# Second expert layer and output in two halves of 256 columns, with all combination weights kept in SBUF

## The chip, the cores and the metric

The kernel runs on one core of a Trainium2 chip. The metric is the device time of one execution in microseconds (us). The kernel before took 548.74 us (median of three runs, 547.72 to 548.89). The profile is of one execution, recorded by the hardware profiler.

Engines are named as the profile names them: PE is the matrix engine (PEld its weight loads), DVE the vector engine, ACT the scalar engine, POOL the GpSimd engine, SP the engine that issues the DMAs.

## The reference, cut to what matters

Thresholded attention over 8 batches, 8 heads, 576 positions, 64 dimensions a head. Its output, as `x` of 4608 tokens by 512 columns, goes through a soft mixture of 8 experts with 4 slots each:

```python
logits = x @ phi                        # 4608 x 32 slots
slot_input = softmax(logits, axis 0).T @ x          # 32 x 512
for e in range(8):
    h = np.maximum(slot_input[e] @ w1[e], 0.0)      # 4 x 1024
    slot_out[e] = h @ w2[e]                         # 4 x 512
c = softmax(logits, axis 1)             # the combination weights, 4608 x 32
return c @ slot_out                     # 4608 x 512
```

`w1` and `w2` are 8 x 1024 x 512 numbers of float32 each, 33.6 MB in all, and the output is 9.44 MB.

## The kernel before, in words

The attention and the slot inputs take the first 483 us, in an order that a planner inside the kernel computes. The change touches only what follows, the tail, whose order is written out by hand: every engine executes its part in program order.

**Weights.** The weights come in 64 units of 512 KB: units 0 to 31 are `w1` (four experts, 128 rows each), units 32 to 63 are `w2` (256 rows of one expert, two rows of 512 columns a partition, so that each partition reads 4 KB in one piece). 46 units fit into SBUF before the tail: 26 in the `w` buffers, loaded during the attention, and 20 in `host` buffers, which take the space of attention buffers as those die. The last `NX = 6` of them, units 12 to 17, lie where the tail's own tiles will lie. The last 18 units, 46 to 63, are loaded by `load_unit` (line 451) into buffers that `stage1` (line 993) and `stage2` (line 1024) have read.

**Layers.** `stage1(a, kb)` multiplies the slot inputs by four units of `w1`, four experts side by side in column groups of 32 on PE. `relu` and `hidden` turn the result into the stationary operand `hz`. `stage2(a, k)` does the second layer in eight steps, each of two rows by four experts; all steps add up in one PSUM tile `so` of 512 columns, and the last step, whose units arrive last, is done in two column halves (`end`). float32 matmuls are two instructions each.

**Combination.** `ct` (line 962) makes one of nine blocks `cT` of combination weights: POOL multiplies (`c_block`), PE transposes, ACT copies, DVE subtracts to split the numbers into two float32r parts. Two blocks are made before the second layer, seven among the output jobs; three buffers hold them. `combine` (line 1054) sums the experts' result over the groups (`sr`), splits it into `sh`, and runs 18 output jobs: two matmuls of 512 columns each (`o`), one result copied out by ACT and one by DVE, and a store of 512 KB in pieces of 4 KB. The last block's two jobs are each stored by two DMAs from 64 partitions.

**Queues.** All DMAs are issued by SP, in program order. `otile` hands out six PSUM tiles in turn for the outputs, three of which the transposes use too.

Of the kernel before, what the change touches and what calls it, by code (L numbers as in the profile page):

```python
# [10 lines left out]
F32 = mybir.dt.float32  # L11
F32R = mybir.dt.float32r
AF = mybir.ActivationFunctionType
ALU = mybir.AluOpType
# [8 lines left out]
    k=2, q=2, vv=2, r=3, ri=3, nmx=4, thr=4, p2=4, pL=1, pTa=1, pTb=1, pTl=1, l4=1,  # L23
# [8 lines left out]
NPRE = 26  # L32
# [3 lines left out]
NHOST = 20  # L36
TABLE = {}
for _n, _v in (
# [78 lines left out]
    TABLE.update({(_n, _i): _x for _i, _x in enumerate(_v) if _x is not None})  # L117
OFF = dict(qk=-1.0, mx=0.0, ex=0.3, th=0.4, st=1.0, ri=1.3, sc=1.5, tt=3.0, te=3.3, tl=3.5, tle=3.8, a0=2.0, a1=5.0,
           ae=0.5, x=6.0, xe=6.3, D=1.0)


class Buf:
# [215 lines left out]
def softmax_attention_soft_moe(  # L338
# [17 lines left out]
    nc = tc.nc  # L356
    B, HP, D, _, S = qT.shape
    NP = B * HP
    N9 = 9
    DM = out.shape[1]  # L360
    E, _, F = w1.shape
    NS = phi.shape[1]
    SPE = NS // E
    SM = 512
# [74 lines left out]
    NG = E // 4  # L439
# [1 line left out]
    units += [(1, 0, 4 * a + g, k) for a in range(NG) for k in range(4) for g in range(4)]  # L441
    wslots = [wp.tile([128, 1024], F32, name=f"w{i}") for i in range(NPRE)]

    NX = 6
    X = range(12, 12 + NX)
    n = NPRE + NHOST
    units = [(i, *units[i]) for i in (*range(X[0]), *range(X[-1] + 1, n), *X, *range(n, len(units)))]
    n_units = len(units)
    where = {}

    def load_unit(t):

        if len(where) == len(units):
            return
        i, kind, _, e, k = units[len(where)]
        where[i] = t
        if kind == 0:
            nc.sync.dma_start(t, w1[e, k * 128:(k + 1) * 128, :])
        else:
            nc.sync.dma_start(t, w2[e, k * 256:(k + 1) * 256, :].rearrange("(p j) f -> p (j f)", j=2))  # L460
# [478 lines left out]
    def ttile(name):  # L939
        return ps_t.tile([128, 512], F32, tag="t", name=name)  # L940

    def two(name, tag):

        return ttile(name + "a"), ps_h.tile([128, 512], F32, tag=tag, name=name + "b")
# [14 lines left out]
    blocks = [(slice(row(b), row(b) + 4), 4) for b in range(B)] + [(slice(N9 - 1, NR, N9), B // 2)]  # L959
    c4s, cTs = [], []  # L960

    def ct():


        if len(cTs) == len(blocks):
            return
        while len(c4s) < min(len(cTs) + 2, len(blocks)):
            c4s.append(c_block(*blocks[len(c4s)]))
        k = blocks[len(cTs)][1]
        c4 = c4s[len(cTs)]  # L970
        n = 128 * k
        t = tx.tile([128, SM], F32R, tag="cT", name=f"cT{len(cTs)}", bufs=3)
        if len(cTs) < 2:
            w = two(f"ct{len(cTs)}", "h00" if cTs else "h01")
            for i in range(k):
                split(w, i, c4[:, i].rearrange("p g s -> p (g s)"))
            tv = t.rearrange("p (i g q) -> p i g q", i=4, g=2)
            for g in range(2):
                wv = w[g][:, 0:256].rearrange("p (i q) -> p i q", i=4)
                nc.scalar.copy(tv[:, :, g], wv)  # L980
                nc.vector.tensor_tensor(
                    out=tv[64:128, :, g], in0=wv[64:128], in1=tv[64:128, :, g].bitcast(F32), op=ALU.subtract)
            cTs.append(t)
            return
        w = ttile(f"ct{len(cTs)}")
        for i in range(k):
            tr(w[:, i * 128:(i + 1) * 128], c4[:, i].rearrange("p g s -> p (g s)"))
        nc.scalar.copy(t[:, 0:n], w[:, 0:n])
        nc.vector.tensor_tensor(  # L989
            out=t[64:128, 0:n], in0=w[64:128, 0:n], in1=t[64:128, 0:n].bitcast(F32), op=ALU.subtract)  # L990
        cTs.append(t)

    def stage1(a, kb, hp):
        t = [where[a * 16 + kb * 4 + g] for g in range(4)]
# [17 lines left out]
    def hidden(a, hid):  # L1012
        for n in range(2):
            w = two(f"ht{a}_{n}", "h10" if a and n else "h00" if n else "h01")
            for k in range(4):
                split(w, k, hid[:, (n * 2 + k // 2) * 256 + k % 2:(n * 2 + k // 2 + 1) * 256:2])
            for g, m in enumerate(rows):
                nc.vector.tensor_tensor(
                    out=hz[:, a, n * 4:(n + 1) * 4, m], in0=w[g][:, 0:256].rearrange("p (k m) -> p k m", k=4),
                    in1=mask[:, a].rearrange("p g s -> p (g s)")[:, None, m].to_broadcast([128, 4, 64]),  # L1020
                    op=ALU.mult,
                )

    def stage2(a, k):
        t = [where[n_units // 2 + a * 16 + k * 4 + g].rearrange("p (j f) -> p j f", j=2) for g in range(4)]

        last = a == NG - 1 and k == 3
        for q, dst in enumerate(end if last else [so]):
            c = slice(q * DM // 2, (q + 1) * DM // 2) if last else slice(0, DM)
            for j in range(2):  # L1030
                for g in range(4):
                    nc.tensor.matmul(
                        dst[g * 32:(g + 1) * 32, 0:c.stop - c.start], hz[:, a, k * 2 + j, g * 32:(g + 1) * 32],
                        t[g][:, j, c], start=(j == 0 and (last or a == 0 and k == 0)),
                        stop=(j == 1 and (last or a == NG - 1 and k == 2)),
                        tile_position=(0, 32 * g), skip_group_check=True)
        for g in range(4):
            load_unit(where[n_units // 2 + a * 16 + k * 4 + g])

    cnt = [-1]  # L1040

    def otile(name):
        cnt[0] += 1
        k = cnt[0] % 6
        return ps_h.tile([128, 512], F32, tag=("h01", "h10", "h11")[k // 2], name=name) if k % 2 else ttile(name)

    def through():

        last = {}
        for i in set(range(n_units)) - set(X):  # L1050
            last[id(where[i])] = (i, where[i])
        return [t for i, t in sorted(last.values(), key=lambda x: x[0])]

    def combine():

        cols = [slice(n * DM // 2, (n + 1) * DM // 2) for n in range(2)]
        for q, w in zip(cols, end):
            nc.vector.tensor_tensor(out=so_sb[:, q], in0=w[:, 0:DM // 2], in1=so_sb[:, q], op=ALU.add)
        for q, x in enumerate(cols):
            w = ttile(f"sr{q}")  # L1060
            nc.tensor.matmul(w[:, 0:DM // 2], st4.rearrange("p g s -> p (g s)"), so_sb[:, x], start=True, stop=True)
            nc.scalar.copy(sh[:, x], w[:, 0:DM // 2])
            nc.vector.scalar_tensor_tensor(
                out=sh[:, x], in0=sh[:, x].bitcast(F32), scalar=neg, in1=w[:, 0:DM // 2], op0=ALU.mult, op1=ALU.add)
        free = through()

        jobs = [(b, k) for b in range(B) for k in (0, 2)] + [(B, k) for k in range(0, B // 2, 2)]
        ov = out.rearrange("(i h s) d -> h s i d", h=2, s=S)
        for n, (b, k) in enumerate(jobs):
            ot = free[n].rearrange("p (c d) -> p c d", c=2)  # L1070
            token = lambda c: slice(k + c, SM, 4) if b < B else slice((k + c) * 128, (k + c + 1) * 128)
            ws = [otile(f"o{n}_{c}") for c in range(2 if n else 0)]
            for q, x in enumerate(cols if n == 0 else []):
                for c in range(2):
                    w = otile(f"o{n}_{c}_{q}")[:, 0:DM // 2]
                    nc.tensor.matmul(w, cTs[b][:, token(c)], sh[:, x], start=True, stop=True)
                    if q:
                        nc.vector.tensor_copy(ot[:, c, x], w)
                    else:
                        nc.scalar.copy(ot[:, c, x], w)  # L1080
            for c in range(len(ws)):
                nc.tensor.matmul(ws[c], cTs[b][:, token(c)], sh, start=True, stop=True)
                if c == 0:
                    nc.scalar.copy(ot[:, c], ws[c])
                else:
                    nc.vector.tensor_copy(ot[:, c], ws[c])  # L1086
            if k:
                ct()
            if b < B:
                nc.sync.dma_start(  # L1090
                    out[b * S:b * S + SM].rearrange("(p c) d -> p c d", c=4)[:, k:k + 2], ot)
            else:
                for h in range(2):
                    nc.sync.dma_start(ov[h, SM:S, k:k + 2], ot[h * 64:(h + 1) * 64])

    hp = [[ps_h.tile([128, 512], F32, tag=f"h{a}{n}", name=f"h{a}_{n}") for n in range(2)] for a in range(NG)]
    hid = []
    so = ps_h.tile([128, 512], F32, tag="so", name="so")
    end = [None, None]
    for a in range(NG):  # L1100
        for kb in range(4):
            stage1(a, kb, hp[a])
# [11 lines left out]
        hid.append(relu(a, hp[a]))  # L1114
    ct()
    ct()
    end[:] = [ps_h.tile([128, 512], F32, tag=t, name=t + "e") for t in ("h00", "h11")]
    for a in range(NG):
        for k in range(4):
            if a == NG - 1 and k == 3:  # L1120
                so_sb = tx.tile([128, DM], F32, name="so_sb")
                nc.scalar.copy(so_sb, so)
            stage2(a, k)
            if a < NG - 1 and k == 1:
                hidden(a + 1, hid[a + 1])
    combine()
    order_all.close()


# [45 lines left out]
```

## Time and profile before

| | before |
|---|---|
| time, median of 3 runs | 548.74 us |
| span of the profiled execution, as its page gives it | 546.2 us |
| PE busy | 527.5 us (97%) |
| DVE, ACT, POOL busy | 471.0, 457.4, 242.1 us |
| HBM read, written | 72.42 MB, 9.44 MB |

The page gives no other time of the profiled execution than its span. Shares of busy time are averages over the whole run. The tail, 483 to 546 us, has limits of its own, and the rows further down are taken from there.

### The profile page before, as it was taken

The numbers are of one execution on the slowest core, as the hardware profiler recorded it, in microseconds if no ns is written. First come the engines' busy times: TensorE is split into PE (matmuls) and PEld (weight loads), VectorE is DVE, ScalarE is ACT, GpSimd is POOL, SyncE is SP. The second block draws the span as 40 slices with busy tenths as digits, with TensorE's granted clock in tenths as the row PEclk, the third lists the DMA queues.
The fourth block names the chain that finished last, engine by engine and source line by source line (L and its number), as shares of the span: only waits on it lengthen the run. The fifth ranks groups of instructions, "written<-read, shape, count | busy, mean of one in ns | idle before, by whom it ended". The sixth has DMA issues, their size and how long they took to land.

```text
span 546.2 us, 18324 instructions
## 1 busy us (share of the span) xinstructions
PE 527.5 (97%) x7029; PEld 337.0 (62%) x7029; DVE 471.0 (86%) x1332; ACT 457.4 (84%) x790; POOL 242.1 (44%) x475
## 2 busy tenths in 40 slices
PE   8999999999999999999999999999999999999990
PEld 6666666666666666666666666666666656644470
DVE  5999998999999999999899989999999999523192
ACT  3899998999899989999999989999999888621181
POOL 2554555554545464545355545545454524121030
PEclk9999999999999999999999999999999999999997
DMA  6355555565535543333333333333333322999498
GB/s 176 74 158 178 168 167 169 138 190 161 166 90 167 172 153 122 92 94 86 78 91 92 91 91 92 91 91 91 91 90 91 91 76 69 336 410 408 197 375 316
DMA packets 31990, 83.03 MB, mean 152 GB/s; under 512 B 4640, under 2 KB 12832, under 8 KB 31904
## 3 DMA queue, kind: packets, MB, share of 16 engines
q1 hardware_dynamic: 31904, 81.87, 48.8%
q8 instruction: 55, 0.90, 0.7%
q14 instruction: 31, 0.25, 0.2%
HBM read 72.42 MB, written 9.44 MB: 150 GB/s over the span
## 4 chain that ended last, share of the span: by engine, by line
PE 82%; DVE 5%; DMA 5%; ACT 4%; issue 2%; DVEq 0%; POOL 0%; SPq 0%; POOLq 0%; ACTq 0%
PE ps L670 29%; PE ps L552 24%; PE ps L478 17%; DMA w<-in_w 5%; PE ps L557 3%; PE ps L694 2%; PE ps L752 2%; PE ps L800 1%; DVE p L580 1%; PE up L418 1%; DVE cT L989 1%; DVE host L1086 1%; ACT pTa L483 1%; DVE ss L564 1%; PE ps L470 1%
## 5 line engine op out<-in xcount | busy, mean ns | idle before, releaser
L564 DVE TENSOR_SCALAR_CACHE_REDUCE ss<-ps 128x576 f32<-128x576 f32 x288 | 209.1, 752 | 15.5 <-ACT pTl L483 4.8
L577 POOL TENSOR_SCALAR thr<-nmx,pabs 128x1 f32<-128x1 f32 x288 | 132.2, 461 | 187.0 <-DVE ss L564 167.7
L580 DVE SCALAR_TENSOR_TENSOR p<-ss,thr,p 128x576 f32<-128x576 f32 x256 | 201.8, 823 | 3.4 <-ACT p L574 3.1
L574 ACT ACTIVATE p<-ss,nmx 128x576 f32<-128x576 f32 x256 | 188.2, 781 | 18.3 <-DVE ss L564 18.2
L552 PE MATMUL ps<-k,q 64*128 64x288 f32 x1024 | 167.2, 427 | 1.0 <-ACT pTb L483 0.4
L478 PE MATMUL ps<-ident,p 64*128 64x64 f32 x2304 | 98.2, 223 | 0.9 <-ACT pTa L483 0.3
L478 PEld LDWEIGHTS ps<-ident,p 64*128 64x128 f32 x2304 | 87.8, 138 | 17.8 <-issue 3.3
L552 PEld LDWEIGHTS ps<-k,q 64*128 64x128 f32 x1024 | 83.3, 188 | 21.9 <-ACT pTl L652 5.8
L483 ACT COPY pTb<-ps 128x1024 f32<-128x1024 f32 (+1 forms) x96 | 84.0, 876 | 5.7 <-PE ps L478 3.5
L670 PE MATMUL ps<-pTb,vv 128*64 128x320 f32 x512 | 76.0, 439 | 0.4 <-DVE pTl L652 0.4
L483 ACT COPY pTa<-ps 128x1024 f32<-128x1024 f32 x64 | 64.9, 1018 | 0.4 <-PE ps L478 0.4
L670 PE MATMUL ps<-pTa,vv 128*64 128x256 f32 x512 | 62.3, 385 | 0.0
L670 PEld LDWEIGHTS ps<-pTb,vv 128*64 128x64 f32 x512 | 34.1, 136 | 36.4 <-issue 9.0
L670 PEld LDWEIGHTS ps<-pTa,vv 128*64 128x64 f32 x512 | 33.9, 136 | 26.2 <-DVE ss L564 8.5
L670 PE MATMUL ps<-pTl,vv 128*64 128x256 f32 (+1 forms) x256 | 41.9, 406 | 0.0
L689 POOL TENSOR_TENSOR x<-x,ri 128x512 f32<-128x512 f32 x31 | 32.3, 1043 | 4.8 <-ACT x L483 4.8
L483 ACT COPY xT<-ps 128x256 f32<-128x256 f32 (+1 forms) x62 | 24.6, 398 | 6.2 <-PE ps L670 5.2
L670 PEld LDWEIGHTS ps<-pTl,vv 128*64 128x64 f32 x256 | 18.5, 137 | 12.6
L580 DVE SCALAR_TENSOR_TENSOR pL<-ss,thr,pL 128x576 f32<-128x576 f32 x32 | 26.0, 812 | 0.0
L574 ACT ACTIVATE pL<-ss,nmx 128x576 f32<-128x576 f32 x32 | 24.8, 776 | 0.4 <-DVE ss L564 0.4
L954 POOL TENSOR_TENSOR c<-lall,crow 128x512 f32<-128x512 f32 x9 | 9.3, 1046 | 35.7 <-PE ct L470 21.4
L483 ACT COPY pTl<-ps 128x256 f32<-128x256 f32 x64 | 24.2, 378 | 0.4 <-PE ps L478 0.4
(165 smaller groups left out, 550.3 us busy)
## 6 DMA issues: line engine op xcount, KB each, us to landing
w<-in_w SPq DMA_DIRECT2D x44, 512.0 KB, 7.3
q<-in_qT SPq DMA_DIRECT2D x62, 288.0 KB, 4.5
vv<-in_vt SPq DMA_DIRECT2D x32, 320.0 KB, 4.6
host<-in_w SPq DMA_DIRECT2D x20, 512.0 KB, 7.8
k<-in_kT SPq DMA_DIRECT2D x62, 144.0 KB, 3.0
out<-w SPq DMA_DIRECT2D x8, 512.0 KB, 3.4
out<-host SPq DMA_DIRECT2D x8, 512.0 KB, 5.0
out<-host SPq DMA_DIRECT2D x4, 256.0 KB, 4.6
```

The costliest lines, as they stand in the source:

```text
L478: nc.tensor.transpose(out=s[:, g, c:c + 64], in_=ins[g], identity=ident[rows[g], rows[g]], tile_position=(64 * g, 0))
L483: G.add("ACT", 51 + 0.833 * n, nom, lambda: nc.scalar.copy(*io()), r, w)
L552: nc.tensor.matmul(s.t[:, g, 0:HS], qt.t[rows[g], h, c * 128:(c + 1) * 128], kt.t[rows[g], h * HS:(h + 1) * HS], start=True, stop=True, ti ...
L557: nc.tensor.matmul(s.t[rows[a], g, 0:HS], qt.t[rows[g], a, SM:S], kt.t[rows[g], a * HS:(a + 1) * HS], start=True, stop=True, tile_position ...
L564: dve(674, t + OFF['mx'], [s], [ss, nmx], lambda s=s, ss=ss, nmx=nmx: nc.vector.tensor_scalar(out=ss.t.rearrange("p (a k) -> p a k", a=2), ...
L574: G.add("ACT", 668, t + OFF['ex'], lambda sv=sv, nmx=nmx, view=view: nc.scalar.activation(view().rearrange("p (a k) -> p a k", a=2), sv(), ...
L577: pool(250, t + OFF['th'], lambda nmx=nmx, thr=thr: nc.gpsimd.tensor_scalar(out=thr.t, in0=nmx.t, scalar1=1.0, scalar2=pabs, op0=ALU.mult, ...
L580: fn=lambda sv=sv, thr=thr, view=view, i=i: nc.vector.scalar_tensor_tensor(out=view().rearrange("p (a k) -> p a k", a=2), in0=sv(), scalar ...
L670: nc.tensor.matmul(lone(w)[h * 64:(h + 1) * 64, 0:n], vv.t[:, v0:v0 + 64], p0, start=(kb == 0), stop=(kb == 4), tile_position=(0, h * 64), ...
L689: G.add("POOL", 1040, u + 6.8, own=f"new{j}", r=[ri[0]], w=[x[j]], fn=lambda: nc.gpsimd.tensor_tensor(out=wide(), in0=wide(), in1=ri.t[:, ...
L694: nc.tensor.transpose(out=w.t[:, g, c * 64:c * 64 + 64], in_=xj()[rows[g], c], identity=ident[rows[g], rows[g]], tile_position=(64 * g, 0))
L752: nc.tensor.matmul(lone(wl)[c * 32:(c + 1) * 32, o], phi_sb[:, k, :], xT[k].t[:, q(c)], start=(k == 0 and not o.start), stop=(k == HP - 1) ...
```

## The change

The second layer is computed in two halves of 256 columns. Its late units are loaded in halves: first the left halves of all 18 late units, then the right halves. Nine buffers take two left halves each, nine others two right halves each. A load is now 256 KB in pieces of 1 KB, and there are 36 of them, all asked for by `stage1`.

`stage2(q, a, k)` does one step for half `q`. All eight steps of half 0 come first. The sum of half 0 is then gathered and spread (`gather`, `spread`), and the eight steps of half 1 are placed among the first output jobs of half 0, in the order that `PLAN0` gives: per entry, a job, the number of half-1 steps ahead of it, and the number of `ct` blocks ahead of it. Then follow jobs 6 and 7 of half 0, the spreading of half 1, job 8 of half 0, and nine jobs of half 1.

An output job is now one block of 512 tokens by 256 columns: four matmuls of 256 columns into two PSUM tiles, one copied out by ACT, one by DVE, and a store of 512 KB in pieces of 1 KB. All nine `cT` blocks have buffers of their own; for these, `NX` is 9 instead of 6. `ct` is cut into `ct_start` and a late part.

```diff
+PLAN0 = ((0, 2, 0), (1, 1, 0), (2, 1, 1), (3, 1, 1), (4, 1, 1), (5, 1, 1), (None, 1, 1))
+REST0 = ((6, 7), (8,))
...
-    NX = 6
+    NX = 9
...
+    halves = [slice(0, 256), slice(256, DM)]
+    units = [(i, *units[i]) for i in (*range(X[0]), *range(X[-1] + 1, n), *X)] + [
+        (i, 2, q, *units[i][2:]) for q in range(2) for i in range(n, n_units, 2)]
...
+        if kind == 2:
+            c = halves[q]
+            v = t[:, 0:4 * (c.stop - c.start)].rearrange("p (e j f) -> p e j f", e=2, j=2)
+            for g in range(2):
+                part[i + g, q] = v[:, g]
+                nc.sync.dma_start(
+                    v[:, g], w2[e + g, k * 256:(k + 1) * 256, c].rearrange("(p j) f -> p j f", j=2))
+            return
...
-        t = tx.tile([128, SM], F32R, tag="cT", name=f"cT{len(cTs)}", bufs=3)
+        t = tx.tile([128, SM], F32R, name=f"cT{n}")
...
+    def stage2(q, a, k):
+        c = halves[q]
+        for j in range(2):
+            for g in range(4):
+                i = n_units // 2 + a * 16 + k * 4 + g
+                t = where[i].rearrange("p (j f) -> p j f", j=2)[:, :, c] if i in where else part[i, q]
+                nc.tensor.matmul(
+                    so[q][g * 32:(g + 1) * 32, 0:c.stop - c.start], hz[:, a, k * 2 + j, g * 32:(g + 1) * 32],
+                    t[:, j], start=(a == 0 and k == 0 and j == 0), stop=(a == NG - 1 and k == 3 and j == 1),
+                    tile_position=(0, 32 * g), skip_group_check=True)
...
+    def job(q, b, pieces=1):
...
+        for m in range(2):
+            w = otile(f"o{q}_{b}_{m}")
+            for c in range(2):
+                k = m * 2 + c
+                token = slice(k, SM, 4) if b < B else slice(k * 128, (k + 1) * 128)
+                nc.tensor.matmul(w[:, c * 256:c * 256 + n], cTs[b][:, token], sh[:, x], start=True, stop=True)
...
+            if m:
+                nc.vector.tensor_copy(ot[:, 2:4], wv)
+            else:
+                nc.scalar.copy(ot[:, 0:2], wv)
...
+                nc.sync.dma_start(out[b * S:b * S + SM].rearrange("(p c) d -> p c d", c=4)[:, c, x], ot[:, c])
...
+    for a, k in steps:
+        stage2(0, a, k)
+        if a < NG - 1 and k == 1:
+            hidden(a + 1, hid[a + 1])
...
+    gather(0)
+    late = [ct_start(), ct_start()]
+    late.pop(0)()
+    spread(0)
+    late.pop(0)()
+    done = iter(steps)
+    for b, ns, nc_ in PLAN0:
+        for _ in range(ns):
+            stage2(1, *next(done))
+        for _ in range(nc_):
+            ct()
+        if b is not None:
+            job(0, b, 2 if b == 0 else 1)
+    gather(1)
+    for b in REST0[0]:
+        job(0, b)
+    while len(cTs) < len(blocks):
+        ct()
+    spread(1)
+    for b in REST0[1]:
+        job(0, b)
+    for b in range(B + 1):
+        job(1, b, 2 if b == B else 1)
```

## Rows read from the trace of the kernel before

**Rows 1.** Busy time by stretch of the tail: stretch and its length, busy time and number of instructions on PE, PEld, DVE, ACT, POOL, granted PE clock (1.00 is 2.4 GHz, 0.50 is 1.2 GHz), busy share of the 16 DMA engines, GB/s.

```profile
483.50:498.90 15.40, 15.40 (x145) 5.45 (x144) 1.42 (x4) 1.79 (x3) 1.74 (x2) 1.00 1.03 410
498.90:513.60 14.70, 14.55 (x157) 5.31 (x153) 2.87 (x8) 2.21 (x6) 2.05 (x2) 1.00 0.90 358
513.60:519.90 6.30, 5.82 (x43) 4.13 (x44) 3.26 (x7) 2.45 (x7) 0.29 (x1) 1.00 0.00 0
519.90:535.00 15.10, 12.86 (x55) 9.56 (x54) 14.48 (x23) 11.99 (x23) 4.94 (x5) 1.00 1.02 406
535.00:546.20 11.20, 0.00 (x0) 0.00 (x0) 0.60 (x2) 0.00 (x0) 0.00 (x0) 0.67 0.83 296
```

**Rows 2.** The chain that ended last, in the tail: start, length, what.

```profile
493.25 10.14 DMA w<-in_w
...
503.45 10.09 DMA w<-in_w
513.54 0.04 issue
513.58 0.83 PE h00e L1032 x9
...
515.50 0.64 PE sr L1061 x2
...
517.20 1.24 PE o L1076 x4
```

**Rows 3.** DMA issues by SP: start, length of the whole run of issues, line, what, count.

```profile
485.40 18.39 SPq L460 DMA_DIRECT2D w<-in_w  x18
519.06 8.10 SPq L1090 DMA_DIRECT2D out<-w  x8
527.73 9.50 SPq L1090 DMA_DIRECT2D out<-host  x8
537.34 4.93 SPq L1094 DMA_DIRECT2D out<-host  x4
```

**Rows 4.** The stores from issue to landing: first line those of 128 and of 64 partitions together, second line the four of 64 partitions alone, whose last issue stands at 541.3.

```profile
DMA to landing us min/median/max: 2.7/4.5/5.2
...
L1094 SPq DMA_DIRECT2D out<-host x4: 955/1214/1345, 537.3 to 541.3; - x4
...
DMA to landing us min/median/max: 3.9/4.6/5.0
```

**Rows 5.** The second layer in the order of time, matmuls (PE) and weight loads (PEld): start, length, line, tile, operands, count. `so` are steps of 512 columns, `h00e` and `h11e` the last step's halves of 256, `ht` the transposes in `hidden`.

```profile
499.55 3.64 PE L1032 MATMUL so<-host,hz 128*32 128x512 f32 x32
503.12 0.33 PE L948 MATMUL ht_0a<-ident,hid 64*128 64x64 f32 x1
...
503.89 0.28 PE L948 MATMUL ht_1a<-ident,hid 64*128 64x64 f32 x1
...
504.01 0.28 PE L948 MATMUL ht_1a<-ident,hid 64*128 64x64 f32 x1
...
504.22 0.64 PE L1032 MATMUL so<-host,hz 128*32 128x512 f32 x4
...
511.54 0.13 PEld L1032 LDWEIGHTS so<-w,hz 128*32 128x32 f32 x4 [0.30 <-issue]
511.97 0.13 PEld L1032 LDWEIGHTS so<-w,hz 128*32 128x32 f32 x4 [0.30 <-issue]
...
513.83 0.11 PEld L1032 LDWEIGHTS h00e<-w,hz 128*32 128x32 f32 x1
...
514.04 0.11 PEld L1032 LDWEIGHTS h00e<-w,hz 128*32 128x32 f32 x1
```

**Rows 6.** The spreading of the result and the output jobs in the order of time, same columns.

```profile
515.43 1.28 PE L1061 MATMUL sr<-so_sb,st 128*128 128x256 f32 x4
...
516.16 0.37 ACT L1062 CAST sh<-sr 128x256 fp32r<-128x256 f32 x1 [2.50 <-PE sr L1061]
...
517.20 1.24 PE L1076 MATMUL o<-sh,cT 128*128 128x256 f32 x4 [0.48 <-DVE sh L1063]
...
518.86 0.60 PE L470 MATMUL ct<-ident,c 128*128 128x128 f32 x4
519.22 1.31 PE L1082 MATMUL o<-sh,cT 128*128 128x512 f32 x4
519.19 1.02 PEld L1082 LDWEIGHTS o<-sh,cT 128*128 128x128 f32 x4
```

**Rows 7.** Groups of instructions between 499 and 537 us: count, busy time in all, mean ns of one.

```profile
L1082 PE MATMUL o<-sh,cT 128*128 128x512 f32 x34 | 11.1, 445 | 0.9 <-DVE cT L989 0.7
L470 PE MATMUL ct<-ident,c 128*128 128x128 f32 x28 | 4.4, 278 | 0.7 <-POOL c L954 0.5
...
L1082 PEld LDWEIGHTS o<-sh,cT 128*128 128x128 f32 x34 | 8.3, 302 | 2.1 <-ACT host L1084 1.8
L470 PEld LDWEIGHTS ct<-ident,c 128*128 128x128 f32 x28 | 3.0, 140 | 2.5 <-POOL c L954 2.1 <-issue 0.3
...
L1084 ACT COPY host<-o 128x512 f32<-128x512 f32 x10 | 5.4, 589 | 1.0 <-PE o L1082 0.8
L1086 DVE COPY host<-o 128x512 f32<-128x512 f32 x10 | 6.3, 686 | 0.1
L989 DVE TENSOR_TENSOR cT<-ct,cT 64x512 fp32r<-64x512 f32 x7 | 4.9, 695 | 0.6 <-ACT cT L988 0.4
```

**Rows 8.** What the DMA queue moved in three stretches, two rows each: all packets, then the share of the 16 engines' time that the queue's packets took. First 520 to 535 us (stores of 4 KB pieces), then 542 to 545 (stores of 2 KB pieces from 64 partitions, the end of the run), then 158.9 to 160.3 (loads of 1152-byte pieces to 64 partitions, beginning on an idle queue).

```profile
DMA packets 1659, 6.08 MB, mean 405 GB/s; under 512 B 176, under 2 KB 176, under 8 KB 1659
q1 hardware_dynamic: 1659, 6.08, 101.6%
...
DMA packets 415, 0.75 MB, mean 250 GB/s; under 512 B 49, under 2 KB 49, under 8 KB 415
q1 hardware_dynamic: 415, 0.75, 73.7%
...
DMA packets 139, 0.15 MB, mean 105 GB/s; under 512 B 11, under 2 KB 139, under 8 KB 139
q1 hardware_dynamic: 139, 0.15, 38.5%
```

More of the change, by code (lines that the diff above doesn't have):

```diff
@@ L442, in softmax_attention_soft_moe @@
     wslots = [wp.tile([128, 1024], F32, name=f"w{i}") for i in range(NPRE)]
-    NX = 6
+    NX = 9
     X = range(12, 12 + NX)
     n = NPRE + NHOST
-    units = [(i, *units[i]) for i in (*range(X[0]), *range(X[-1] + 1, n), *X, *range(n, len(units)))]
     n_units = len(units)
-    where = {}
+    halves = [slice(0, 256), slice(256, DM)]
+    units = [(i, *units[i]) for i in (*range(X[0]), *range(X[-1] + 1, n), *X)] + [
+        (i, 2, q, *units[i][2:]) for q in range(2) for i in range(n, n_units, 2)]
+    where, part, sent = {}, {}, []
     def load_unit(t):
-        if len(where) == len(units):
+        if len(sent) == len(units):
             return
-        i, kind, _, e, k = units[len(where)]
+        i, kind, q, e, k = units[len(sent)]
+        sent.append(t)
+        if kind == 2:
[6 more added lines that the diff above has]
+            return
         where[i] = t
@@ L960, in softmax_attention_soft_moe, with ct_start @@
     c4s, cTs = [], []
[L962 to L967, printed above, removed]
+    def ct_start():
+        n = len(cTs)
+        while len(c4s) < min(n + 2, len(blocks)):
             c4s.append(c_block(*blocks[len(c4s)]))
-        k = blocks[len(cTs)][1]
-        c4 = c4s[len(cTs)]
-        n = 128 * k
-        t = tx.tile([128, SM], F32R, tag="cT", name=f"cT{len(cTs)}", bufs=3)
-        if len(cTs) < 2:
-            w = two(f"ct{len(cTs)}", "h00" if cTs else "h01")
+        k = blocks[n][1]
+        c4 = c4s[n]
+        t = tx.tile([128, SM], F32R, name=f"cT{n}")
+        cTs.append(t)
+        if n < 2:
+            w = two(f"ct{n}", "h00" if n else "h01")
             for i in range(k):
@@ L977, in ct, with late @@
             tv = t.rearrange("p (i g q) -> p i g q", i=4, g=2)
[L978 to L985, printed above, removed]
+            def late():
+                for g in range(2):
+                    wv = w[g][:, 0:256].rearrange("p (i q) -> p i q", i=4)
+                    nc.scalar.copy(tv[:, :, g], wv)
+                    nc.vector.tensor_tensor(
+                        out=tv[64:128, :, g], in0=wv[64:128], in1=tv[64:128, :, g].bitcast(F32), op=ALU.subtract)
+            return late
+        w = ttile(f"ct{n}")
+        n = 128 * k
         for i in range(k):
             tr(w[:, i * 128:(i + 1) * 128], c4[:, i].rearrange("p g s -> p (g s)"))
[L988 to L991, printed above, removed]
+        def late():
+            nc.scalar.copy(t[:, 0:n], w[:, 0:n])
+            nc.vector.tensor_tensor(
+                out=t[64:128, 0:n], in0=w[64:128, 0:n], in1=t[64:128, 0:n].bitcast(F32), op=ALU.subtract)
+        return late
+    def ct():
+        ct_start()()
     def stage1(a, kb, hp):
@@ L1022, in hidden @@
                 )
[L1024 to L1038, printed above, removed]
+    def stage2(q, a, k):
[8 more added lines that the diff above has]
+                    tile_position=(0, 32 * g), skip_group_check=True)
     cnt = [-1]
@@ L1045, in otile @@
         return ps_h.tile([128, 512], F32, tag=("h01", "h10", "h11")[k // 2], name=name) if k % 2 else ttile(name)
[L1047 to L1088, printed above, removed]
@@ new lines, in gather, with spread @@
+    def gather(q):
+        nc.scalar.copy(so_sb[:, halves[q]], so[q][:, 0:halves[q].stop - halves[q].start])
+    def spread(q):
+        x = halves[q]
+        w = ttile(f"sr{q}")[:, 0:x.stop - x.start]
+        nc.tensor.matmul(w, st4.rearrange("p g s -> p (g s)"), so_sb[:, x], start=True, stop=True)
+        nc.scalar.copy(sh[:, x], w)
+        nc.vector.scalar_tensor_tensor(
+            out=sh[:, x], in0=sh[:, x].bitcast(F32), scalar=neg, in1=w, op0=ALU.mult, op1=ALU.add)
+    ov = out.rearrange("(i h s) d -> h s i d", h=2, s=S)
@@ new lines, in job @@
+    def job(q, b, pieces=1):
+        x = halves[q]
+        n = x.stop - x.start
+        ot = free.pop(0)[:, 0:4 * n].rearrange("p (c d) -> p c d", c=4)
+        for m in range(2):
[4 more added lines that the diff above has]
+                nc.tensor.matmul(w[:, c * 256:c * 256 + n], cTs[b][:, token], sh[:, x], start=True, stop=True)
+            wv = w.rearrange("p (c d) -> p c d", c=2)[:, :, 0:n]
+            if m:
+                nc.vector.tensor_copy(ot[:, 2:4], wv)
+            else:
+                nc.scalar.copy(ot[:, 0:2], wv)
+            if (m + 1) * pieces % 2:
+                continue
+            c = slice(2 * m if pieces == 2 else 0, 2 * m + 2)
@@ L1089, in combine @@
             if b < B:
-                nc.sync.dma_start(
-                    out[b * S:b * S + SM].rearrange("(p c) d -> p c d", c=4)[:, k:k + 2], ot)
+                nc.sync.dma_start(out[b * S:b * S + SM].rearrange("(p c) d -> p c d", c=4)[:, c, x], ot[:, c])
             else:
                 for h in range(2):
-                    nc.sync.dma_start(ov[h, SM:S, k:k + 2], ot[h * 64:(h + 1) * 64])
+                    nc.sync.dma_start(ov[h, SM:S, c, x], ot[rows[h], c])
     hp = [[ps_h.tile([128, 512], F32, tag=f"h{a}{n}", name=f"h{a}_{n}") for n in range(2)] for a in range(NG)]
@@ L1097, in softmax_attention_soft_moe @@
     hid = []
-    so = ps_h.tile([128, 512], F32, tag="so", name="so")
-    end = [None, None]
     for a in range(NG):
@@ L1116, in softmax_attention_soft_moe @@
     ct()
[L1117 to L1126, printed above, removed]
+    so = [ps_h.tile([128, 512], F32, tag="so", name="so0")]
+    steps = [(a, k) for a in range(NG) for k in range(4)]
+    for a, k in steps:
+        stage2(0, a, k)
+        if a < NG - 1 and k == 1:
+            hidden(a + 1, hid[a + 1])
+    so.append(ps_h.tile([128, 512], F32, tag="h00", name="so1"))
+    so_sb = tx.tile([128, DM], F32, name="so_sb")
+    free = [where[i] for i in range(27, 32)]
+    free += sent[NPRE + NHOST:NPRE + NHOST + 9] + [where[i] for i in range(32, NPRE + NHOST)]
+    gather(0)
[21 more added lines that the diff above has]
+        job(1, b, 2 if b == B else 1)
     order_all.close()
```

## Prediction

> **What bounds the kernel now.** I read the stretches of the tail first [rows 1], then the chain that ended last [rows 2], then the queue of stores [rows 3, 4]. Up to 513.6 us the DMA engines are full (share 1.03, 410 GB/s): 46 units have been asked for and the 18 late ones follow, 1.28 us each, so the late ones begin near 513.54 - 18 x 1.28 = 490.5. PE is as full as they are: 15.40 of 15.40 and 14.55 of 14.70 us. The chain names the last load as what ended last, at 513.54, but PE had hardly any slack behind it. Then the DMA engines stand still for 6.3 us (0 GB/s from 513.6 to 519.9) while the result is finished, spread and multiplied. From 519.9 on they are full again with stores: 405 GB/s, 1.295 us for 512 KB. The first store is issued at 519.06 and lands 2.7 us later; 15 more follow at 1.295, and the last MB, from 64 partitions, takes about 4.0: 519.06 + 2.7 + 19.4 + 4.0 = 545.2, which is also 541.3 + 3.9, the last issue and its landing. So the tail is load, hole, store. Removing the hole alone is worth at most 6.3 us.
>
> The sum is made against the profiled span, 546.2 us, 1.0 us of which lies behind the last landing. The median, 548.74, is 2.5 us above the span; I carry the difference of the spans over to it.
>
> **Half 0 of the second layer.** A group of four weight loads stands 0.43 us behind the last one at 512 columns and 0.21 at 256 [rows 5]. A step is four groups: 1.72 before, 0.86 a half. Halving costs PE nothing. From 499.55, eight half steps (6.9), `hidden` in between (503.12 to 504.22, 1.1) and one change of kind (0.1) end half 0 at T0 = 507.7. The left halves come from 490.5 on and are all there by 504 even at the dearer price below; the DMAs set nothing here. `NX` = 9 puts unit 20 last among the 46. It is there at 490.5, and `stage1` reaches it after five steps of 1.72, at 492.1: nothing.
>
> **From T0 to the seventh store.** The PE queue is in program order, so this is a sum.
> - Seven `ct` (blocks 2 to 8). Four transposes take 0.60 from the first's start to the last's end, and one is 0.27 long [rows 6, 7], so they follow each other by 0.11: 0.44 each `ct`, 3.1.
> - `spread(0)`: 0.6.
> - Eight half-1 steps: 6.9. Their weights are long there: the last right half lands by 513.5 to 518, step 7 is reached at about 524.
> - Seven jobs of four matmuls. At 512 columns four weight loads take 1.02, of which the last is 0.30 [rows 6, 7], so they follow each other by 0.24. A matmul of 256 columns cannot hide that load (the four in `L1076` took 1.24): 0.95 a job, 6.7. A job now moves as many bytes as before with four weight loads instead of two.
> - Changes of kind. A batch of four `ct` and four `o` took 519.22 + 1.31 - 518.86 less 0.17 (a matmul's record of about 0.4, 0.24 of which is its turn): 1.50, which is 0.11 over their own 0.44 + 0.95; `so` to `ht` is 0.13 late, `ht` to `so` 0.09 [rows 5]. I count 20 changes (three per round of step, `ct`, job) at 0.13: 2.6. At nothing each they would cost 0, and no row speaks for more than 0.2, 4.0.
>
> Together 19.9, so job 6 leaves PE at 527.6. Drain, the DVE copy (0.69) and the issue add 0.95: its store is issued at 528.55.
>
> ACT and DVE each have about 0.6 to 0.7 for a job and as much for a `ct` [rows 7], 1.4 in a round of 2.6; they hide. `gather(0)` makes ACT wait for PE; behind it stand block 2's copy and `sh`. `sh` is ready at about 510.4 and job 0 reaches PE at 511.1 behind two half-1 steps, which cover it; without them job 0 would start 0.9 later than PE could. POOL's multiplications have 2.6 each. SP's 36 loads are all released by `stage1` and have until 524, over 1 us each (18 took 18.4 before, paced by landings [rows 3]); the stores behind them in its queue are not ready before 513.
>
> **The DMAs.** Loads of 1 KB pieces, and stores of 1 KB pieces, are not in this trace. The lower end is the price at 4 KB, 1.295 per 512 KB; nothing about smaller pieces speaks for a gain. The stretch of 2 KB stores has 0.737 x 3 us x 16 / 366 = 97 ns a packet, 1.55 per 512 KB, but from 64 partitions and at a run's end. The loads of 1152 bytes have 0.385 x 1.4 x 16 / 128 = 67 ns, at 1 KB some 60, or 1.92 per 512 KB, with an idle queue's start in it [rows 8]. I take 1.42, half-way between the first two.
>
> By the Trainium skill, page DMA: Bandwidth & Descriptors, section Specifications, pieces of 512 B and up run at line rate. No stretch here shows that for 1 KB, and the two nearest speak against it; by the rule the time would be 550.5. The same page's section Why small descriptors are slow (HBM only) gives a fixed 3 cycles a packet beside 32 bytes a cycle: 4 x 35 / 131, an estimate of 7% more, which would make 551.4.
>
> With 1.42 the loads end at 490.5 + 25.6 = 516.1. Six stores are ready between 513 and 526, 2.6 apart, so the queue idles some 4 us of the 12.5 up to the seventh. From there PE makes a job a microsecond and the queue is full: 528.55 + 2.7 + 9 x 1.295 + 4.0 = 546.9, plus 1.25 for ten halves in 1 KB pieces and 0.25 on the last MB: 548.4. Against 545.2 that is +3.2. The hole is not removed; it is moved into the gaps between the first six stores, where PE is late, and the smaller pieces are paid on top. **Forecast: 548.74 + 3.2 = 551.9 us.** With 1.295 and 1.55 it is 550.4 and 553.5.
>
> **Rivals.**
> - *PE keeps up (the other side).* If PE hides the changes of kind and the weight loads of one matmul under the one before, a round is 2.0 instead of 2.6. It decides where the seventh store is issued: at the price of 1.42 the kernel breaks even when PE needs 16.6 us instead of 19.9. For it: transposes' loads take 0.14 rather than 0.30 [rows 7] and follow at 0.11. Against it: the 0.24 stands in every full batch. Without the 2.6, and with pieces at 4 KB's price, 551.9 - 2.6 - 1.5 = 547.8; with job loads at 0.14 as well, 2.8 less, 545.0. Chance 0.27, three quarters of it under 547.6.
> - *Small pieces are dear.* At 1.7 per 512 KB the queue never idles: loads end at 521.1, sixteen halves at 548.3, the last MB with its landing at 554.1, so 557.6. For it: the 67 ns. Against it: the idle start in that row. At 1.92 it would be about 566. Chance 0.13.
> - *The whole hole is filled (what the change says).* Six jobs would have to be ready at the queue's pace, 1.4 apart instead of 2.6: loads to 516.1, then sixteen halves and the last MB, 516.1 + 22.7 + 4.3 + 0.5 = 543.6, or 547.1. A step alone is 0.86, so it needs the whole of the first rival; it is inside its chance.
>
> **Chances and range.** Forecast 0.60 (own range 549.9 to 554.5), PE keeps up 0.27, dear pieces 0.13. What a measurement can tell from no change is 0.2%, 1.1 us: 547.6 to 549.8. Faster 0.20, within 0.19 (the rest of the first rival and the forecast's edge), slower 0.61. The range reaches from 546.0, leaving out the best tenth, to 556.5, leaving out most of the dear pieces.
>
> **What would show it.** The last matmul of half 0 near 507.5, PE without idle time from 499 to 527, the first six stores issued 2.6 us apart, DMA share well under 1 between 517 and 528, full stores from 529. GB/s in that last stretch gives the piece's price: 370 for my 1.42. I am wrong if the stores follow the last load without a gap, if four weight loads of a job take under 0.8, or if the granted clock, 1.00 here until the jobs end, is lower among them.

## The result, and the profile after

The changed kernel took 552.26 us (median of six runs, 551.89 to 552.59), beside 548.29 for six runs of the kernel before (547.06 to 549.00): a ratio of 1.0073, 95% interval 1.006 to 1.0086. It is 0.7% slower, inside the range, and 0.4 us from the forecast. The profiled execution took 552.23 us with a span of 550.5 (before 546.2).

The stretches of the tail of the kernel after answer to [rows 1]; the columns are the same.

```profile
core 0: us, PE busy (x) PEld busy (x) DVE busy (x) ACT busy (x) POOL busy (x), PEclk, DMA share, GB/s
483.50:498.90 15.40, 15.40 (x160) 5.51 (x152) 1.42 (x4) 2.23 (x4) 1.48 (x2) 1.00 1.07 368
498.90:507.50 8.60, 8.60 (x152) 5.24 (x147) 2.87 (x8) 1.36 (x6) 2.05 (x2) 1.00 1.06 340
507.50:516.00 8.50, 8.50 (x89) 5.82 (x88) 3.25 (x5) 3.33 (x7) 2.40 (x3) 1.00 1.09 350
516.00:528.50 12.50, 12.38 (x108) 9.27 (x108) 7.67 (x12) 6.32 (x14) 2.78 (x3) 1.00 0.75 260
528.50:549.00 20.50, 8.22 (x36) 8.02 (x36) 7.05 (x11) 5.59 (x10) 0.00 (x0) 0.81 0.96 307
```

PE has no idle time from 483 to 528 and its granted clock is 1.00 throughout (the 2.4 GHz level). The stretch with 0 GB/s has gone. In its place stands one of 12.5 us at a DMA share of 0.75: some 3.1 us of standing still, in pieces. Before it the share is full at 340 to 350 GB/s, where [rows 1] has 410.

The chain that ended last, kernel after, answers to [rows 2]: start, length, what.

```profile
502.00 5.32 PE so L1051 x96
507.31 1.02 PE ct L485 x8
508.34 0.43 PE sr L1069 x2
508.77 1.86 PE so L1051 x32
510.63 1.14 PE o L1086 x4
...
514.91 0.59 PE ct L485 x4
515.50 0.94 PE o L1086 x4
516.44 1.00 PE so L1051 x16
...
525.61 1.87 PE o L1086 x8
527.48 0.45 PE sr L1069 x2
...
528.89 7.76 PE o L1086 x32
...
536.68 0.69 DVE w L1089
```

No load and no store stands in it: from the last matmul of half 0 (507.31) it is PE, step, `ct`, job, in rounds of 1.00 + 0.59 + 0.94 = 2.53 us. From 537 on it tells nothing of the end, since the stores are then only waiting for each other.

The DMA issues by SP, kernel after, answer to [rows 3].

```profile
484.28 28.11 SPq L468 DMA_DIRECT2D w<-in_w  x36
512.62 16.34 SPq L1096 DMA_DIRECT2D out<-w  x9
529.50 1.95 SPq L1099 DMA_DIRECT2D out<-w  x2
531.55 10.98 SPq L1096 DMA_DIRECT2D out<-w  x8
542.62 4.95 SPq L1099 DMA_DIRECT2D out<-host  x4
```

The last load lands at 517.7. The first store is issued at 512.62, but behind loads, and lands only at 518.3. The nine DMAs of the first eight jobs (job 0 has two) take 16.3 us to be issued; from job 2 on they stand 2.53 apart, as PE makes the jobs. The store of job 6, the seventh, is the mark in all that follows: issued at 527.74, landed 3.3 us later, at 531.0. From there the queue has work until the last landing at 549.55 (before: 545.2), which is 21.8 us after that issue. The lines of that store's issue and of its landing, first the kernel after, then, in a fence of its own, the kernel with stores in 4 KB pieces (below):

```profile
527.74 0.53 SPq L1096 DMA_DIRECT2D out<-w  x1
...
DMA to landing us min/median/max: 3.3/3.3/3.3
```

```profile
527.89 0.33 SPq L1098 DMA_DIRECT2D out<-w  x1
...
DMA to landing us min/median/max: 2.6/2.6/2.6
```

The queue's account of the 4.35 us between the last landings: the loads end 4.1 later (517.66 for 513.54); the standing still behind them is 3.1 for 6.4 (513.54 to 519.9), 3.3 less; what is left is the time of the stores, 28.8 for 25.3, 3.5 more. 4.1 - 3.3 + 3.5 = 4.3. The 3.1 is an estimate from the mean share of the 16 engines, (1 - 0.75) x 12.5.

### The profile page after: what moved, and what is told of

The parts are those of the page before. It is cut to its first block, busy times and chain, and to the rows that moved or that the text cites. A ratio compares the mean times of both kernels' runs of the same rounds, so it can differ in the third digit from the quotient of the medians.

```text
span 550.5 us, 18637 instructions
## 1 busy us (share of the span) xinstructions
PE 531.7 (97%) x7175; PEld 346.1 (63%) x7175; DVE 470.0 (85%) x1329; ACT 457.6 (83%) x790; POOL 241.2 (44%) x475
## 4 chain that ended last, share of the span: by engine, by line
PE 89%; ACT 4%; DVE 3%; issue 1%; DVEq 0%; POOL 0%; POOLq 0%; ACTq 0%
PE ps L685 29%; PE ps L567 24%; PE ps L493 17%; PE ps L572 3%; PE o L1086 3%; PE so L1051 3%; PE h L1018 3%; PE ps L709 2%; PE ps L767 2%; PE ps L815 1%; DVE p L595 1%; ACT pTa L498 1%; DVE ss L579 1%; PE up L422 1%; PE ps L485 1%
## 5 line engine op out<-in xcount | busy, mean ns | idle before, releaser
L547 POOL TENSOR_SCALAR k<-k,flag 128x576 f32<-128x576 f32 x31 | 24.0, 776 | 1.8 <-DMA k<-in_kT 1.5
```

The lines of the kernel that those rows point to most:

```text
L547: sc = lambda e, kc=kc: lambda: e.tensor_scalar(out=kt.t[:, kc], in0=kt.t[:, kc], scalar1=flag8, **one)
```

## The experiments

The theory: PE's sum sets when the seventh store is issued; from there a full queue, whose price is that of 1 KB pieces, sets the end; the dearer loads are hidden. The leftover is the last block's job, whose stores go from 64 partitions at a time. Each kernel is the change with one edit, unless its text says otherwise. The table has the results first: the median and the runs of the kernel before on the same chip beside it, the ratio with its 95% interval, the issue of the seventh store and the last landing in the profiled execution, all in us.

| | time | before | ratio | seventh store | last landing | between |
|---|---|---|---|---|---|---|
| the change | 552.26 | 548.29 | 1.0073 (1.006 to 1.0086) | 527.74 | 549.55 | 21.8 |
| loads in 4 KB | 552.58 | 547.86 | 1.0088 (1.0073 to 1.0103) | 527.97 | 549.91 | 21.9 |
| stores in 4 KB | 549.84 | 547.86 | 1.0037 (1.0023 to 1.0052) | 527.89 | 547.07 | 19.2 |
| both in 4 KB | 550.31 | 548.10 | 1.0039 (1.0026 to 1.0052) | 527.66 | 546.95 | 19.3 |
| five `ct` left out | 550.02 | 547.86 | 1.0041 (1.0026 to 1.0056) | 525.56 | 547.35 | 21.8 |
| steps first | 554.03 | 547.86 | 1.0114 (1.0099 to 1.0129) | 530.02 | 551.85 | 21.8 |
| steps first, loads in 4 KB | 551.26 | 548.50 | 1.0055 (1.0037 to 1.0072) | 526.43 | 548.36 | 21.9 |
| leftover of half 0 in 128 KB | 551.67 | 548.10 | 1.0065 (1.0052 to 1.0078) | 527.70 | 549.02 | 21.3 |
| leftover of half 1 first | 552.04 | 548.50 | 1.0059 (1.0039 to 1.0079) | 528.26 | 549.70 | 21.4 |
| four blocks in halves | 548.50 | 548.10 | 1.0009 (1.0000 to 1.0019) | - | 545.62 | - |

Where only the order on PE or the loads differ, the last column stands at 21.8 to 21.9 while the seventh store moves over 4.5 us. Where only the stores' pieces differ, the seventh store stands within 0.3 us and the last column moves.

### Pieces of 4 KB: loads, stores, both

Loads: each late unit is read whole by one DMA, so that a load is 512 KB in 4 KB pieces.

```diff
-                nc.sync.dma_start(
-                    v[:, g], w2[e + g, k * 256:(k + 1) * 256, c].rearrange("(p j) f -> p j f", j=2))
+            nc.sync.dma_start(t, w2[e + q, k * 256:(k + 1) * 256, :].rearrange("(p j) f -> p (j f)", j=2))
```

> Theory (PE paces the first seven stores, so the late loads have slack): the nine pairs of late loads are 18 loads of 512 KB in 4 KB pieces (other weights, so the output is not the reference's); the loads end some 3.5 us earlier, near 513.6 instead of 517.1, the seventh store is issued at the same time, near 527.7, and the time stays at 552.3, within 0.5. Rival (the DMA queue's work in small pieces sets the end, loads and stores alike): about 3.4 us less, 548.8.

Stores: each job's rows go to one contiguous range of the output.

```diff
-                nc.sync.dma_start(out[b * S:b * S + SM].rearrange("(p c) d -> p c d", c=4)[:, c, x], ot[:, c])
+                m = c.stop - c.start
+                o0 = b * S + q * 256 + c.start * 64
+                nc.sync.dma_start(
+                    out[o0:o0 + 64 * m].rearrange("(p r) d -> p (r d)", p=128),
+                    ot[:, c].rearrange("p c d -> p (c d)"))
```

> The stores of 512 KB from 128 partitions go to other places of the output, in one piece of 4 KB a partition (the output is permuted). Theory: only the stores behind the seventh count, nine halves at 1.30 instead of 1.45 and 0.5 less from issue to landing of the first: 1.5 to 2 us less, 550.5. If PE paces nothing and the queue is all, loads still at 1 KB: 16 halves x 0.15, 2.4 less, 549.9. If the price of 1 KB stores is nothing: 552.3.

> Late loads and main stores both in 4 KB pieces (other weights and a permuted output). Theory (PE paces the first seven stores): loads in 4 KB pieces give nothing on top of the stores, the seventh store stays near 527.8, and the time is that of the stores alone, 549.8 within 0.5. Rival (pieces on both sides add up): 549.8 - 3.4 = 546.4.

Loads in 4 KB gave nothing. Two stretches of that kernel, columns as above:

```profile
507.50:516.00 8.50, 8.50 (x92) 5.82 (x89) 3.25 (x5) 3.23 (x7) 2.17 (x3) 1.00 0.70 267
516.00:528.50 12.50, 12.50 (x109) 9.50 (x108) 7.53 (x11) 6.32 (x14) 3.00 (x3) 1.00 0.61 210
```

The DMA share falls from 1.09 and 0.75 to 0.70 and 0.61: the queue only stands still longer, while PE is as busy as it was and the seventh store comes no earlier. Stores in 4 KB gave 2.4 us by the medians, 2.0 by the distance to the runs of before beside each. The time alone does not choose between the theory (1.5 to 2 less) and its rival in which PE paces nothing (2.4 less, 549.9): 549.84 is the rival's number. The trace does: the seventh store is issued where it was (527.89 for 527.74), in rounds of PE as before. Both in 4 KB gave no more than the stores alone (550.31, at the upper edge of what was expected). The price of the loads is hidden, that of the stores is paid.

What the queue moved shows the price. First the kernel after while half 1's stores run (537 to 541 us, then 541 to 545); then, in a fence of its own, the kernel with stores in 4 KB (535 to 541).

```profile
DMA packets 1435, 1.42 MB, mean 356 GB/s; under 512 B 45, under 2 KB 1435, under 8 KB 1435
...
DMA packets 1401, 1.39 MB, mean 348 GB/s; under 512 B 43, under 2 KB 1401, under 8 KB 1401
```

```profile
DMA packets 678, 2.47 MB, mean 411 GB/s; under 512 B 74, under 2 KB 76, under 8 KB 678
```

At 352 GB/s, 512 KB take 1.49 us; at 411, 1.28. Nine halves behind the seventh store at 0.21 each are 1.9 us of the 2.6 by which the last column differs; the rest is the seventh store's own way from issue to landing, 2.6 for 3.3. These stores go to one contiguous range each, where those of the change do not, but that is not what helps: the stores of the kernel before, 4 KB pieces at a distance of 8 KB, moved 405 GB/s [rows 8].

### Five `ct` left out

Jobs 4 to 8 read the blocks 0 to 3 again, so that PE has less to do before the seventh store.

```diff
+    cTs += [cTs[i % 4] for i in range(len(cTs), len(blocks))]
     for b, ns, nc_ in PLAN0:
...
-        for _ in range(nc_):
-            ct()
...
-    while len(cTs) < len(blocks):
-        ct()
```

> Five of the nine blocks of combination weights are not made; jobs 4 to 8 read blocks 0 to 3 again (so these rows of the output are wrong). Bytes moved are the same. Theory: PE loses 5 x 0.59 ahead of the seventh store, which is issued near 524.8 instead of 527.7; the queue, idle for about 3.1 us between 516 and 528.5, takes most of it: 2.3 to 3 us less, near 549.6. Rival (the queue sets the end, not PE): 552.3, within 0.5.

The chain of that kernel:

```profile
512.93 1.14 PE o L1086 x4
514.07 1.00 PE so L1051 x16
515.07 1.14 PE o L1086 x4
516.21 1.00 PE so L1051 x16
```

A round is 2.14 instead of 2.53. The seventh store is issued 2.2 earlier and the kernel ends 2.2 earlier. PE paces the first seven stores, and a microsecond saved there is a microsecond at the end. The size is a little below what was expected: without a `ct` between them a job behind a step takes 1.14 instead of 0.94, so leaving out 0.59 gains only 0.39.

### All steps of half 1 ahead of the first job

```diff
-PLAN0 = ((0, 2, 0), (1, 1, 0), (2, 1, 1), (3, 1, 1), (4, 1, 1), (5, 1, 1), (None, 1, 1))
+PLAN0 = ((0, 8, 0), (1, 0, 0), (2, 0, 1), (3, 0, 1), (4, 0, 1), (5, 0, 1), (None, 0, 1))
```

> All eight half-1 steps stand ahead of the first output job of half 0. Theory: the sum on PE up to the seventh store is the same less some 12 changes of kind at 0.14, so that store comes about 1.7 earlier although the first six come later (the first near 518.6 instead of 512.6): 550.5. Rival (the stores' start behind the loads sets the end): the queue idles from 517 to about 519.4 where it was fed before, 2.3 us more, 554.5.

The time is 3.5 us above my theory's number and near the rival's. The chain of that kernel has a wait that I had not counted:

```profile
512.74 5.74 DMA w<-in_w
518.49 0.04 issue
518.53 1.05 PE so L1051 x10
519.58 2.08 PE o L1086 x8
```

The last right half lands at 518.49, and PE, which by its order has only these steps to do, waits for it. The first store is issued at 520.90 instead of 512.62. I had taken the loads as hidden, and they are, but it is the jobs between the steps that hide them. Whether it was this or the order itself was tried with the same order and loads in 4 KB:

> As with all half-1 steps ahead of the first output job, and in addition each late load takes 4 KB pieces (the same number of bytes of other weights, so the result is left with wrong weights in the late units). Theory on why that order cost 1.8 us more than the change: PE ran out of right halves and waited for the last one, which landed at 518.5 because 1 KB loads take 1.48 us per 512 KB instead of 1.28. With 4 KB pieces the loads end about 3.5 us earlier, near 514.5; PE reaches the last steps at about 513, so a wait of a microsecond or so is left of 5.7, the seventh store is issued near 527 to 528 instead of 530.0, and the time is 551 to 552.3 us. Rival (the order itself costs PE the time, by changes of kind or by ct blocks that bunch behind the steps): the seventh store stays near 530 and the time at 554.

```profile
508.94 7.04 PE so L1050 x128
515.98 2.08 PE o L1085 x8
518.06 0.44 PE ct L484 x4
518.50 0.95 PE o L1085 x4
```

It was the loads. The eight steps follow each other without a wait (the last load lands at 513.25), and the seventh store is issued 3.6 us before that of the same order with 1 KB loads. It comes at 526.43, earlier than the 527 to 528 that I expected, and in this lies a second finding: against the change's order with 4 KB loads (527.97) the seventh store is 1.5 earlier. Steps in one batch take 7.04 / 8 = 0.88 each and a `ct` behind a job 0.44, where the mixed order pays 1.00 and 0.59. So mixing steps among the jobs costs 1.5 us on PE, and pays for it by hiding the 1 KB loads. The first theory was right on PE (1.7 expected) and wrong on the loads.

### The leftover block

The last block's stores go from 64 partitions each. In the change, half 0's are two DMAs of 256 KB and half 1's four of 128 KB. One kernel cuts those of half 0 into four DMAs of 128 KB which alternate between the two halves of the partitions; another puts half 1's leftover ahead of half 1's other jobs.

```diff
-        job(0, b)
+        job(0, b, 2 if b == B else 1)
```

> The last block of half 0 is stored by four DMAs of 128 KB, from partitions 0 to 63 and 64 to 127 in turn, instead of two of 256 KB. Theory (a store from 64 partitions is slow because it leaves half of the SBUF side unused, and short ones in turn overlap): its 3.4 us fall to about 2.5, 0.9 less, 551.3. Rival (the price is the small piece alone): 552.3 or a little more for two more issues.

```diff
-    for b in range(B + 1):
-        job(1, b, 2 if b == B else 1)
+    for b in (B, *range(B)):
+        job(1, b, 2 if b == B - 1 else 1)
```

> The change with half 1's job for the last block (the one whose stores go to 64 partitions each) put ahead of half 1's other eight jobs, so that the run ends with stores from all 128 partitions. Theory: a store to 64 partitions costs about 2 us more of the queue's time than one of 128 partitions wherever it stands, so moving it gains nothing in the middle, and only the small end differs: 551.5 to 552.5 us. Rival (it is dear only at the end, where nothing runs beside it): 550.3 to 551.

The kernel after, 532.6 to 536.0 us, where half 0's leftover goes out, and 545.7 to 549.6, its end; then the end of the kernel before, 541.4 to 545.2; last, the end of the kernel with half 1's leftover first, 545.8 to 549.7, whose last job is stored from 128 partitions.

```profile
DMA packets 969, 0.96 MB, mean 283 GB/s; under 512 B 44, under 2 KB 968, under 8 KB 968
...
DMA packets 804, 0.74 MB, mean 190 GB/s; under 512 B 80, under 2 KB 804, under 8 KB 804
```

```profile
DMA packets 487, 0.87 MB, mean 228 GB/s; under 512 B 64, under 2 KB 64, under 8 KB 487
```

```profile
DMA packets 1046, 1.02 MB, mean 260 GB/s; under 512 B 55, under 2 KB 1046, under 8 KB 1046
```

Against the rate of the stores around them (352, and 405 before) the stretches lose 3.4 x (1 - 283 / 352) = 0.7, 3.9 x (1 - 190 / 352) = 1.8 and 3.8 x (1 - 228 / 405) = 1.7 us. Not all of what an end loses is the leftover's: the last fence, with full stores at the end, loses 3.9 x (1 - 260 / 352) = 1.0 us too, so that of the 1.8 some 0.8 is left for the leftover, about what it costs in the middle. The kernel before loses this once, at its end; the change loses as much at its end and 0.7 in the middle besides.

Alternating halves gave 0.6 us by the medians (0.4 by the ratios, whose intervals overlap, so the times alone do not show a gain) and 0.5 between seventh store and end, where the change and the four kernels that differ from it only in the order on PE, in the `ct` or in the loads lie within 0.2 of each other; expected was 0.9. The other order gained 0.4 between seventh store and end, and its seventh store came 0.5 later; its time lies in the theory's range, and without that delay it would be 551.5, still in it. The leftover's four stores took 4.9 us in the middle of the run, where 1 MB of full stores takes 3.0: it is dear there too. It is not the short DMA that is dear: that kernel's last job goes out in two DMAs of 256 KB from 128 partitions, and they land 0.7 us apart.

In the kernel before, the same cut of the last block (eight DMAs of 128 KB) was tried:

```diff
-                for h in range(2):
-                    nc.sync.dma_start(ov[h, SM:S, k:k + 2], ot[h * 64:(h + 1) * 64])
+                for c in range(2):
+                    for h in range(2):
+                        nc.sync.dma_start(ov[h, SM:S, k + c], ot[h * 64:(h + 1) * 64, c])
```

> The kernel before with its last block stored by eight DMAs of 128 KB from the two halves of the partitions in turn, instead of four of 256 KB. Theory as for the last: the last MB falls from about 4.0 us to 2.9, held by SP's issues of some 0.6 each: 0.5 to 1 us less than the kernel before, 547.3. Rival (small pieces alone): no change, or slower by the four issues.

548.25 beside 548.10, ratio 1.0008 (1.0000 to 1.0016): nothing. The gain that I expected did not come: the last MB took 4.3 us, for 3.9 before, with the last issues now 0.6 to 0.7 apart. Why 64 partitions are slow was not settled.

### Nine blocks of combination weights alone

```diff
-    NX = 6
+    NX = 9
...
-        t = tx.tile([128, SM], F32R, tag="cT", name=f"cT{len(cTs)}", bufs=3)
+        t = tx.tile([128, SM], F32R, name=f"cT{len(cTs)}")
```

> The kernel before with only NX = 9 and a buffer of its own for each of the nine cT blocks. Theory: both are free of cost and of gain, because no wait for a cT buffer stands in the chain of the kernel before and the units moved back are long there when stage1 reaches them: the time of the kernel before, within 0.5 us. Rival (three units moved to the end of the first 46 make stage1 wait, or a ct waits less for a buffer): a difference of 1 us or more.

548.93 beside 548.50, ratio 1.0006 (0.9992 to 1.0021). This part of the change costs and gains nothing that can be measured.

### Four blocks in halves, the rest in 512 columns

Only as many jobs of 256 columns as are needed while half 1 is unfinished; the other five blocks go out as in the kernel before. Its core:

```diff
-PLAN0 = ((0, 2, 0), (1, 1, 0), (2, 1, 1), (3, 1, 1), (4, 1, 1), (5, 1, 1), (None, 1, 1))
+PLAN0 = ((0, 2, 0), (1, 2, 0), (2, 2, 0), (None, 2, 0))
...
+    for b in range(4):
+        job(1, b, 2 if b == 0 else 1)
+    for b in range(4, B + 1):
+        for k in (0, 2):
...
+                nc.tensor.matmul(w, cTs[b][:, token], sh, start=True, stop=True)
```

> Second layer in halves and loads in halves as in the changed kernel, but only blocks 0 to 3 are put out in halves; blocks 4 to 8 follow in 512 columns, with stores of 4 KB pieces as before. Theory: four jobs and no ct ahead of the end of half 1 instead of six jobs and five ct, so half 1's first store comes near 524.4 and the queue idles about 2.4 us instead of 3.1 and has eight halves in 1 KB pieces instead of eighteen: the last landing comes back to about 545.3, as in the kernel before, 548 within 1. Rival (the halved second layer itself costs): over 550.

Two stretches of it:

```profile
516.00:528.50 12.50, 12.40 (x90) 10.49 (x82) 7.25 (x12) 7.15 (x14) 2.67 (x3) 1.00 0.79 270
528.50:549.00 20.50, 4.91 (x22) 3.54 (x20) 7.03 (x11) 5.03 (x10) 0.42 (x1) 0.71 0.81 296
```

The DMA engines stand still about as long as in the change (share 0.79), but the run of stores behind it is again one of 4 KB pieces, 1.30 apart, with one leftover. That brings 3.8 us by the medians and the time of the kernel before, not less.

## Why the prediction was right, and what in it was off

The place, the sign and the mechanism held. The closeness of the number is in part luck: the last landing was 1.15 us later than predicted (549.55 for 548.4), and the profiled execution's time lay 1.7 us above its span, where I had carried 2.5 over from the kernel before.

- *Half 0 costs PE nothing by halving.* Right to 0.2 us: it took 8.3 for 8.1. That it ended at 507.31 for 507.7 has another reason: it began at 498.96, where the kernel before began at 499.55 [rows 5]. I had not foreseen that, and why it did is open.
- *The sum on PE to job 6, 19.9.* It was 19.2 (507.31 to 526.55: the two jobs at 525.61 in 1.87). The term that was off is the 20 changes of kind: 2.6 predicted, and 1.9 left, if the other terms stand. The rows say where they lie. Behind a step, a `ct` takes 0.59 and a job 1.14; behind a job, a step takes 1.00; in a batch of their own kind they take 0.44, 0.97 and 0.88. A job behind a `ct` takes 0.94: that change is free. So five of the changes that I counted, those from a `ct` to a job, cost nothing, and the others 0.12 to 0.17.
- *Weight loads of a job not hidden by 256 columns.* Right: 0.94 for 0.95 behind a `ct`, 0.97 in a batch, where weight loads fill 8.02 of PE's 8.22 us. With this the rival in which PE keeps up fell; its rounds would have been 2.0, and they were 2.53.
- *Six stores 2.6 apart, the queue standing still some 4 us of 12.5.* Right: 2.53 from job 2 on, and a share of 0.75, 3.1 us.
- *Seventh store at 528.55.* It came at 527.74, 0.8 earlier: PE 1.05, less a drain and issue of 1.2 instead of 0.95.
- *Price of a 1 KB store, 1.42.* The mark that I had named, 370 GB/s, was 352: 1.49. Eleven stores' worth of bytes behind the seventh at 0.07 each are 0.8 us too little. It is the step that was mis-sized first. The rule of the Trainium skill, page DMA: Bandwidth & Descriptors, section Specifications, that pieces of 512 B and up run at line rate, is not what these runs show (352 beside 411 GB/s); the estimate of 7% by the same page's fixed cost per packet, section Why small descriptors are slow (HBM only), is less than half of the 17% measured.
- *The last MB, 4.25.* I priced the leftover once, at the end. Its half in the middle of the run costs 0.7 besides, and this was not in the sum. A store's way from issue to landing was 3.3 for 2.8 (0.4). So 0.8 + 0.7 + 0.4 - 0.8 = 1.1 of the 1.15.
- *Loads to 516.1, hidden.* They ended at 517.7 and were hidden, as loads in 4 KB show. That the cover is the jobs between the steps I learned only from the order without them.
- *NX and the buffers, nothing.* Right.
- *Dear pieces, 557.6.* It needed 1.7 per 512 KB; it was 1.49, and the queue did stand still.
- *Slips in the sums.* At 1.295 a store my terms give 550.4, not also 550.5, and the break-even of PE is 16.7, not 16.6. A round is 2.25 without changes of kind and 1.86 with the cheap weight loads as well; 2.0 is neither. None of these moves the forecast.

## What to carry to other kernels

A gap on one resource is worth closing only as far as the engine that feeds it has slack: here PE was full on both sides of the gap, so of the 6.4 us of standing still 3.1 came back between the first stores, and the finer pieces that this took were then paid over the whole run of stores behind it. Keep the fine form to the part that needs it (four blocks in halves took the time of the kernel before, nine 4 us more), and when work is interleaved to fill one gap, ask what it hides elsewhere before it is put in order again.

## What was not expected of the hardware

- On a full queue stores of 512 KB in 1 KB pieces moved 348 to 356 GB/s, in 4 KB pieces 405 to 411. Loads in 1 KB pieces moved 340 to 350, in 4 KB pieces 410 [rows 1], but there the DMA was half as long too (256 KB for 512 KB), so that the piece is not shown alone.
- On PE a change between steps (column groups of 32) and jobs or transposes (full width) cost 0.12 to 0.17 us, one from transposes to jobs nothing (0.94 behind a `ct`, 0.97 in a batch). That the width is the cause was not tested by itself.
- While stores from 64 partitions ran, the whole queue's rate was lower: 283 GB/s in the middle of a run that has 352 around it, at a busy share of 0.98.
